# Block-causal attention with eight routed experts on one core: early row gathers in turns with weight pieces, and expert 3's rows gathered among the results

## The chip, the core and the metric

The kernel runs on one core of a Trainium2 chip: TensorE (matmul; in the profile PE, its weight loads PEld), VectorE (DVE), ScalarE (ACT), GpSimd (POOL) and SyncE (SP), and 16 DMA engines that all queues share. The metric is the time of one execution on the device in microseconds; smaller is better. The kernel before took 266.24 us, the median of three runs (264.31 to 266.30).

## The reference

Two stages. First, causal attention by blocks of 64: 8 batches, 8 heads, 576 positions, head size 64. Its result is laid out as 4608 token rows of 512 values. Second, each token row goes through the expert that `domain_id` names, one of 8:

```python
scores = np.where(block_i >= block_j, scale * q @ k.T, -1e9)   # blocks of 64 positions
x = softmax(scores) @ v        # -> rows (4608, 512)
...
for e in range(E):
    mask = domain_id == e
    h = np.maximum(x[mask] @ w1[e], 0.0)      # (512, 1024)
    out[mask] = h @ w2[e]                     # (1024, 512)
```

## The kernel before

**Attention** runs in 32 steps, one for a pair of heads that share a batch (`for p in range(npair + 1)`, L580). In a step TensorE makes scores, ScalarE exponentials (L398), TensorE the product with v (L435, L446), VectorE the normalisation into the tile `x` (L459). When four steps (a batch) are done, its rows are stored to a buffer in device memory, `x_rows` (`store_x`, L465), by SyncE's queue and partly ScalarE's.

**Routing** is worked out beside attention: a table `tok0` holds for each expert 5 blocks of 128 token numbers. It is built so that blocks 0 to 2 of an expert hold only tokens of the first five batches ("early" blocks), and blocks 3 and 4 the rest.

**Gathers.** Rows go from `x_rows` into an expert's tile `xg` (four buffers) by an indirect DMA of 128 rows that GpSimd issues. `early_gather` (L528) reads an early block with row numbers that `early_row` (L524) has copied; it waits only for the first five batches. `gather` (L489) waits for all stores. GpSimd also issues every load of weights (each expert has w1 and w2, each in two halves of 128 x 2 x 1024 or the like, converted from four bytes to two on the way, list `todo`) and every result, an indirect DMA that scatters 128 rows to the output (L735). So GpSimd's instruction list is one queue for rows, weights and results; what stands behind a waiting instruction waits too. Each of its DMAs also waits for the one eight places earlier.

**What sets the order around the change.** All is written out by hand. The dict `issue` (L574) tells what GpSimd issues at the end of attention step p: a pair (e, w) is the early gather of block w of expert e, any integer is the next piece of weights from `todo`. After step 31 the calls from L780 on follow: further early gathers, then late blocks of experts 0 to 2 in turns with weights (`run(...)`, L786), then the two matmul stages of experts 0 and 1. These two are cut in an early part (blocks 0 to 2, `mm1_part` and `mm2` with `range(NE)`) and a late part (blocks 3 and 4). `mm1_part` (L704) is rows times w1 with ReLU on ScalarE into `hT`; `mm2` (L717) is `hT` times w2, one block of 128 tokens at a time, copied to `osb` (ten buffers) and scattered. The dict that `mm2` gets lists what GpSimd issues behind each block's result.

**Turning rows.** Matmuls need the rows turned (`xT`, three buffers). For expert 0's early blocks TensorE does it in the last two attention steps (`early_blocks`, L510), for the others of experts 0 and 1 TensorE does it too (`transpose_block`, L670, `turn_late`, L767), and from expert 2 on VectorE, 16 transposes of 32 x 32 blocks for an expert (`turn`, L674). Experts 2 to 7 are a loop (L810): turn the next expert, then mm1 and mm2 of this one; results of expert e go in turns with rows and weights of later experts (`beside_results`, L756). The last loop (L821), for experts with more than 640 tokens, runs no round here.

Of the kernel before, what the change touches and what calls it, by code (L numbers as in the profile page):

```python
# [17 lines left out]
def kernel(  # L18
# [16 lines left out]
    NB = 5  # L35
# [5 lines left out]
    NE = 3  # L41
# [437 lines left out]
    def weights(e):  # L479
        where = (msb, 1) if e % (NW + 1) == NW else (wsb, NW)  # L480
        w1s[e], w2s[e], todo = load_weights(moe_w1[e], moe_w2[e], *where)
        return todo
# [6 lines left out]
    def gather(g, tok, blks):  # L489
        for blk in blks:  # L490
            nc.gpsimd.indirect_dma_start(  # L491
                out=g[:, blk, :], out_offset=None, in_=xd,
                in_offset=bass.IndirectOffsetOnAxis(
                    ap=tok[:, 1, blk : blk + 1], axis=0),
                bounds_check=N - 1, oob_is_err=False)

    def new_xg():
        return gsb.tile([128, NB, DM], F16, name="xg", tag="xg", bufs=4)
# [25 lines left out]
    def early_row(e, w):  # L524
        rows[e, w] = const.tile([128, 1], I32, name=f"row{e}{w}")
        nc.vector.tensor_copy(out=rows[e, w][:], in_=tok_of(e)[:, 1, w : w + 1])  # L526

    def early_gather(e, w):  # L528
        row = rows[e, w]
        nc.gpsimd.indirect_dma_start(  # L530
            out=xgs[e][:, w, :], out_offset=None, in_=xd[0 : N - LB * S],
            in_offset=bass.IndirectOffsetOnAxis(ap=row[:, 0:1], axis=0),
            bounds_check=N - LB * S - 1, oob_is_err=False)
# [32 lines left out]
    def turn_qk(*at):  # L566
        if at in Ts:
            G, s = Ts[at]
            if s == 0 and G > 1:
# [1 line left out]
            emit_T(G, s, beside.get(at[0]) if at[1] else None)  # L571

    prev, full, halves = None, [], []
    issue = {22: (0, 0), 24: ((0, 0), (0, 1)), 25: ((0, 2), 0), 26: ((1, 0), 0),  # L574
             27: ((1, 1), 0), 28: ((1, 2), 0), 30: ((2, 0),), 31: ((2, 1),)}

    def tok_of(e):
        return tok0[:, :, NB * e : NB * e + NB]

    for p in range(npair + 1):  # L580
# [63 lines left out]
            xgs = [new_xg() for _ in range(4)]  # L644
            xT = new_xT()
        if p == npair - 1:
            early_row(2, 2)
            for w in range(NE):
                early_row(3, w)
        for g in issue.get(p, ()):  # L650
            if isinstance(g, int):
                todo.pop(0)()
# [17 lines left out]
    def transpose_block(g, xT, blk):  # L670
        pt = new_po()[:, 0:256].bitcast(F16).rearrange("p (c n) -> p c n", c=4)
        transpose_to(pt, g, xT, blk)
# [91 lines left out]
    def dst_of(e):  # L764
        return outs[NB * e : NB * e + NB]

    def turn_late(g, xT):  # L767
        for blk in range(NE, NB):
            transpose_block(g, xT, blk)

    def rows_of(e, *blks):
        if len(xgs) <= e:
            xgs.append(new_xg())
        return [lambda blk=blk: gather(xgs[e], tok_of(e), (blk,)) for blk in blks]

    def run(*fs):
        for f in fs:
            f()

    early_gather(2, 2)  # L780
    W1, W2 = todo, weights(2)
    g0, g1, g2, g3 = (rows_of(e, *range(NE, NB)) for e in range(4))
    early_gather(3, 0)
    early_gather(3, 1)
    early_gather(3, 2)
    run(g0[0], W1[0], g0[1], W1[1], g1[0], W2[0], g1[1], g2[0], W2[1], g2[1])  # L786
    hT0, hT1, xT0, xT1, xT2 = new_hT(), new_hT(), xT, new_xT(), new_xT()
    mm1_part(xT0, hT0, w1s[0], 0, CE)
    mm2(hT0, w2s[0], tok_of(0), dst_of(0), range(NE),
        {0: [W2[2]], 1: [g3[0], W2[3]], 2: [g3[1]]},  # L790
        more={n: [lambda n=n: transpose_block(xgs[1], xT1, n)
                  for n in ((0,), (1, 2))[n]] for n in range(2)})
    mm1_part(xT1, hT1, w1s[1], 0, CE, lambda: turn_late(xgs[0], xT0))
# [1 line left out]
    W, g4 = weights(3), rows_of(4, *range(NB))  # L795
    mm1_part(xT0, hT0, w1s[0], CE, CAP - CE)
    mm2(hT0, w2s[0], tok_of(0), dst_of(0), range(NE, NB),
        {0: [g4[0], W[0]], 1: [g4[1], W[1]]})
    mm2(hT1, w2s[1], tok_of(1), dst_of(1), range(NE),
        {0: [g4[2], W[2]], 1: [g4[3], W[3]], 2: [g4[4]]},  # L800
        more={0: [lambda: turn_late(xgs[1], xT1)]})
    turn(xgs[2], xT2, NE, NB)
    mm1_part(xT1, hT1, w1s[1], CE, CAP - CE)
    W, g5 = weights(4), rows_of(5, 0, 1, 2)
# [71 lines left out]
```

## Time and profile before

| | |
|---|---|
| median of three runs (range) | 266.24 us (264.31 to 266.30) |
| the profiled execution | 264.74 us, span 263.0 us, granted TensorE clock 0.991 |
| TensorE busy | 246.5 us (94%) |
| VectorE, ScalarE, GpSimd busy | 179.4, 161.7, 170.0 us |
| GpSimd's DMA queue | 60192 packets, 45.63 MB |
| DMA rate, mean over the span | 193 GB/s |
| attention until about | 111.8 us |

The span is the time from the first to the last instruction; the run's own time is 1.7 us longer. Share of busy time is an average: attention and experts are two stages with different limits, so the views below are read by stretch of time. GpSimd's busy time in the profile is the time in which it writes a DMA's list, not the time of the transfer.

### The profile page before, as it was taken

To read this page: it belongs to the slowest core of one execution; us is meant where nothing else is said; L and a number is where in the kernel's file an instruction comes from. 1 tells how busy PE (TensorE), PEld (TensorE's weight loads), DVE (VectorE), ACT (ScalarE), POOL (GpSimd) and SP (SyncE) were. 2 spreads that over 40 slices of the span, in tenths; PEclk is the share of its full clock that TensorE was granted. 3 is DMA by queue.
4 is the path that set the end of the run, shared out by engine and by line. 5 is a ranking of instruction groups with operands and counts; after the bars stand their busy time and mean duration, and the time that the engine had idled before them with its cause. 6 is when DMAs were issued, how large, how long until landed. Compare 5 with 4: busy or idle time off the path is not lost. (4 is left out here: it accounts for less than half of the span.)

```text
span 263.0 us, 7025 instructions
## 1 busy us (share of the span) xinstructions
PE 246.5 (94%) x2918; PEld 156.6 (60%) x2918; DVE 179.4 (68%) x306; ACT 161.7 (62%) x201; POOL 170.0 (65%) x200
## 2 busy tenths in 40 slices
PE   7799999999999999898999999999999999999970
PEld 5466666666667666654565675564654745646540
DVE  4779998999977866511597899996959949600010
ACT  1669998999999889724443464463553644635420
POOL 8698965747485557365888888678888864042150
PEclk9999999999999999999999999999999999999996
DMA  5999999999999999994999999999999999022030
GB/s 79 156 171 183 208 176 228 188 214 197 204 214 198 209 204 260 251 268 73 218 241 275 211 262 259 228 258 238 264 207 258 224 230 289 27 100 80 2 149 34
DMA packets 65889, 50.85 MB, mean 193 GB/s; under 512 B 41277, under 2 KB 54077, under 8 KB 65856
## 3 DMA queue, kind: packets, MB, share of 16 engines
q0 software_dynamic: 60192, 45.63, 101.1%
q1 hardware_dynamic: 5120, 4.33, 6.1%
q8 instruction: 24, 0.39, 0.6%
q10 hardware_dynamic: 544, 0.43, 0.5%
q14 instruction: 9, 0.07, 0.1%
HBM read 67.15 MB, written 15.20 MB: 313 GB/s over the span
## 5 line engine op out<-in xcount | busy, mean ns | idle before, releaser
L398 ACT ACTIVATE A<-ps 128x1024 f16<-128x1024 f32 x96 | 92.2, 1023 | 11.2 <-PE ps L393 4.3
L679 DVE STREAM_TRANSPOSE xT<-xg 32x640 f16<-32x640 f16 (+2 forms) x112 | 82.9, 741 | 11.3 <-DMA xg<-x_rows,tok 7.4
L725 PE MATMUL po<-w2h,hT 128*128 128x512 f16 (+1 forms) x328 | 71.4, 374 | 0.7 <-DMA xg<-x_rows,row 0.6
L735 POOL DMA_INDIRECT out_dram<-osb,tok x40 | 40.5, 1013 | 36.4 <-ACT osb L732 22.1
L725 PEld LDWEIGHTS <-hT 128*128 128x128 f16 x328 | 31.8, 98 | 36.3 <-ACT hT L714 1.7
L696 PE MATMUL ph<-xT,w1h 128*128 128x320 f16 x384 | 53.1, 299 | 0.1
L732 ACT COPY osb<-po 128x512 f32<-128x512 f32 (+1 forms) x39 | 22.6, 581 | 45.6 <-PE po L725 37.5
L696 PEld LDWEIGHTS <-w1h 128*128 128x128 f16 x384 | 37.6, 98 | 15.8 <-issue 0.4
L700 ACT ACTIVATE hT<-ph 128x640 f16<-128x640 f32 x48 | 33.8, 704 | 19.1 <-PE ph L696 15.0
L383 DVE COPY QK<-PT 128x1152 f16<-128x1152 f16 x30 | 40.5, 1351 | 4.5 <-PE ps L393 1.5
L393 PE MATMUL ps<-QK 64*128 64x64 f16 (+3 forms) x320 | 39.0, 295 | 1.8 <-ACT A L398 1.1
L95 POOL DMA_DIRECT2D vS<-in_v_dram x44 | 35.7, 831 | 3.1 <-DMA kh<-in_k_dram 1.6
L491 POOL DMA_INDIRECT xg<-x_rows,tok x28 | 29.1, 1039 | 12.0 <-issue 6.4
L435 PE MATMUL po<-vS,A 128*128 128x65 f16 x640 | 28.9, 195 | 1.3 <-DVE x L459 1.0
L435 PEld LDWEIGHTS <-A 128*128 128x128 f16 x640 | 23.1, 98 | 10.6 <-issue 7.9
L459 DVE TENSOR_TENSOR x<-po,rc 128x640 f16<-128x640 f32 x32 | 26.4, 824 | 1.1
L446 PE MATMUL po<-vS,A 64*64 64x65 f16 (+1 forms) x320 | 21.0, 194 | 0.4 <-DMA vS<-in_v_dram 0.3
L730 DVE COPY osb<-po 128x512 f32<-128x512 f32 (+1 forms) x2 | 1.1, 558 | 26.5 <-issue 25.5
L530 POOL DMA_INDIRECT xg<-x_rows,row x12 | 12.3, 1028 | 9.6 <-DVE row L526 5.2
L711 PE MATMUL ph<-xT,w1h 128*128 128x384 f16 (+1 forms) x128 | 18.4, 299 | 0.1
L76 POOL DMA_DIRECT2D qh<-in_q_dram x15 | 11.0, 731 | 11.2 <-DMA kh<-in_k_dram 9.5
L714 ACT ACTIVATE hT<-ph 128x768 f16<-128x768 f32 (+1 forms) x16 | 11.1, 704 | 11.1 <-PE ph L711 8.7
(109 smaller groups left out, 192.2 us busy)
## 6 DMA issues: line engine op xcount, KB each, us to landing
w1h<-in_moe_w_dram POOLq DMA_DIRECT2D x16, 512.0 KB
w2h<-in_moe_w_dram POOLq DMA_DIRECT2D x16, 512.0 KB
qh<-in_q_dram POOLq DMA_DIRECT2D x15, 288.0 KB
kh<-in_k_dram POOLq DMA_DIRECT2D x15, 288.0 KB
x_rows<-x SPq DMA_DIRECT2D x6, 512.0 KB
vS<-in_v_dram POOLq DMA_DIRECT2D x24, 128.0 KB
vS<-in_v_dram POOLq DMA_DIRECT2D x24, 64.0 KB
out_dram<-osb,tok POOLq DMA_INDIRECT x40
```

What stands on the lines that cost most here:

```text
L95: nc.gpsimd.dma_start(out=vS[b % RV][r0:128, c, h0:h1, 16:80], in_=v[b, h0:h1, 128 * c : 128 * c + n, :].rearrange("h p d -> p h d"))
L383: nc.vector.tensor_copy(out=QKs[G][:, s].rearrange("p i (n j) -> p i n j", j=R), in_=P16.rearrange("p (j i n) -> p i n j", j=R, i=2))
L393: nc.tensor.matmul(out=o[:, t], lhsT=QK[h, 1, i, 128 * c : 128 * c + 128], rhs=QK[h, 0, i, q0:q1], start=True, stop=True)
L398: nc.scalar.activation(out=o, in_=i, func=AF.Exp, scale=0.125)
L435: nc.tensor.matmul(out=po[:, t, 65 * w : 65 * w + 65], lhsT=st["A"][:, t, n0 : n0 + 128], rhs=vS[b % RV][:, c, head(st, t), 15:80], start= ...
L459: nc.vector.tensor_tensor(out=st["x"][:, :, c0 : c0 + 256].rearrange("p w (t i z) -> p i t w z", t=2, i=2)[:, st["i"]], in0=po[:, :, 0:325 ...
L491: nc.gpsimd.indirect_dma_start(out=g[:, blk, :], out_offset=None, in_=xd, in_offset=bass.IndirectOffsetOnAxis(ap=tok[:, 1, blk : blk + 1], ...
L679: nc.vector.transpose(out=dst[32 * j : 32 * j + 32, i, b0:b1], in_=src[32 * i : 32 * i + 32, j, b0:b1])
L696: nc.tensor.matmul(out=ph[:, i, 0:w], lhsT=w1_cols(w1h, dc, fc), rhs=xT[:, dc, w * i : w * i + w], start=(dc == 0), stop=(dc == 3))
L700: nc.scalar.activation(out=hT[:, fc, :].rearrange("p (i n) -> p i n", i=2), in_=ph[:, :, 0:w], func=AF.Relu)
L725: nc.tensor.matmul(out=po[:, 0:w], lhsT=hT[:, fc, 128 * blk : 128 * blk + 128], rhs=w2h[:, fc, w * i : w * i + w], start=(fc == 0), stop=( ...
L735: nc.gpsimd.indirect_dma_start(out=dst[blk], out_offset=bass.IndirectOffsetOnAxis(ap=tok[:, 0, blk : blk + 1], axis=0), in_=osb[:], in_off ...
```

## The change

It changes three things, and no arithmetic.

1. `issue`: in steps 24 to 28 one early gather and one piece of weights stand in each step. The first half of expert 0's w1 stays in step 22, the second goes from there behind the first early gather; expert 0's third block and all of experts 1 and 2 follow one step or place later than before.
2. Expert 3 loses its three early gathers after step 31 (and the copies of their row numbers); expert 2's second block joins the third there.
3. Expert 3 gets all five blocks by ordinary gathers behind the results of experts 0 and 1 (`g3` has five entries), and expert 4's five blocks follow behind them.

```diff
--- before.py
+++ after.py
@@ -571,8 +571,8 @@
             emit_T(G, s, beside.get(at[0]) if at[1] else None)
 
     prev, full, halves = None, [], []
-    issue = {22: (0, 0), 24: ((0, 0), (0, 1)), 25: ((0, 2), 0), 26: ((1, 0), 0),
-             27: ((1, 1), 0), 28: ((1, 2), 0), 30: ((2, 0),), 31: ((2, 1),)}
+    issue = {22: (0,), 24: ((0, 0), 0), 25: ((0, 1), 0), 26: ((0, 2), 0),
+             27: ((1, 0), 0), 28: ((1, 1), 0), 30: ((1, 2),), 31: ((2, 0),)}
 
     def tok_of(e):
         return tok0[:, :, NB * e : NB * e + NB]
@@ -644,9 +644,8 @@
             xgs = [new_xg() for _ in range(4)]
             xT = new_xT()
         if p == npair - 1:
-            early_row(2, 2)
-            for w in range(NE):
-                early_row(3, w)
+            for w in (1, 2):
+                early_row(2, w)
         for g in issue.get(p, ()):
             if isinstance(g, int):
                 todo.pop(0)()
@@ -777,17 +776,16 @@
         for f in fs:
             f()
 
+    early_gather(2, 1)
     early_gather(2, 2)
     W1, W2 = todo, weights(2)
-    g0, g1, g2, g3 = (rows_of(e, *range(NE, NB)) for e in range(4))
-    early_gather(3, 0)
-    early_gather(3, 1)
-    early_gather(3, 2)
+    g0, g1, g2, g3 = (
+        rows_of(e, *range(NE if e < 3 else 0, NB)) for e in range(4))
     run(g0[0], W1[0], g0[1], W1[1], g1[0], W2[0], g1[1], g2[0], W2[1], g2[1])
     hT0, hT1, xT0, xT1, xT2 = new_hT(), new_hT(), xT, new_xT(), new_xT()
     mm1_part(xT0, hT0, w1s[0], 0, CE)
     mm2(hT0, w2s[0], tok_of(0), dst_of(0), range(NE),
-        {0: [W2[2]], 1: [g3[0], W2[3]], 2: [g3[1]]},
+        {0: [g3[0], W2[2]], 1: [g3[1], W2[3]], 2: [g3[2]]},
         more={n: [lambda n=n: transpose_block(xgs[1], xT1, n)
                   for n in ((0,), (1, 2))[n]] for n in range(2)})
     mm1_part(xT1, hT1, w1s[1], 0, CE, lambda: turn_late(xgs[0], xT0))
@@ -795,9 +793,9 @@
     W, g4 = weights(3), rows_of(4, *range(NB))
     mm1_part(xT0, hT0, w1s[0], CE, CAP - CE)
     mm2(hT0, w2s[0], tok_of(0), dst_of(0), range(NE, NB),
-        {0: [g4[0], W[0]], 1: [g4[1], W[1]]})
+        {0: [g3[3], W[0]], 1: [g3[4], W[1], g4[0]]})
     mm2(hT1, w2s[1], tok_of(1), dst_of(1), range(NE),
-        {0: [g4[2], W[2]], 1: [g4[3], W[3]], 2: [g4[4]]},
+        {0: [g4[1], W[2], g4[2]], 1: [g4[3], W[3]], 2: [g4[4]]},
         more={0: [lambda: turn_late(xgs[1], xT1)]})
     turn(xgs[2], xT2, NE, NB)
     mm1_part(xT1, hT1, w1s[1], CE, CAP - CE)
```

On GpSimd, at attention steps 22 to 30 (L530 is an early gather, L127 and L132 are halves of w1 and w2, expert 0's, then expert 1's w1). Before:

```order
L127 DMA w1h_2051<-in_moe_w1_dram 128x2x1024 x2
L530 DMA xg_2229<-x_rows,row00_2234 128x512
L530 DMA xg_2229<-x_rows,row01_2239 128x512
L530 DMA xg_2229<-x_rows,row02_2316 128x512
L132 DMA w2h_2052<-in_moe_w2_dram 128x2x1024
L530 DMA xg_2230<-x_rows,row10_2393 128x512
L132 DMA w2h_2052<-in_moe_w2_dram 128x2x1024
L530 DMA xg_2230<-x_rows,row11_2471 128x512
L127 DMA w1h_2227<-in_moe_w1_dram 128x2x1024
L530 DMA xg_2230<-x_rows,row12_2552 128x512
L127 DMA w1h_2227<-in_moe_w1_dram 128x2x1024
```

And now:

```order
L127 DMA w1h_2051<-in_moe_w1_dram 128x2x1024
L530 DMA xg_2228<-x_rows,row00_2233 128x512
L127 DMA w1h_2051<-in_moe_w1_dram 128x2x1024
L530 DMA xg_2228<-x_rows,row01_2311 128x512
L132 DMA w2h_2052<-in_moe_w2_dram 128x2x1024
L530 DMA xg_2228<-x_rows,row02_2388 128x512
L132 DMA w2h_2052<-in_moe_w2_dram 128x2x1024
L530 DMA xg_2229<-x_rows,row10_2466 128x512
L127 DMA w1h_2226<-in_moe_w1_dram 128x2x1024
L530 DMA xg_2229<-x_rows,row11_2547 128x512
L127 DMA w1h_2226<-in_moe_w1_dram 128x2x1024
L530 DMA xg_2229<-x_rows,row12_2670 128x512
```

The second half of w1 stands behind the first early gather, and each gather of experts 0 and 1 behind a piece of weights.

On GpSimd, from step 31 to the first late blocks (L491 is a gather that waits for all stores of attention rows; `xg_2231` before and `xg_2230` now are expert 2's rows, `xg_2229` now expert 1's). Before, six early gathers stand here from step 30 on, the last three for expert 3 (`xg_2232`):

```order
L530 DMA xg_2231<-x_rows,row20_2675 128x512
L530 DMA xg_2231<-x_rows,row21_2751 128x512
L530 DMA xg_2231<-x_rows,row22_2743 128x512
L530 DMA xg_2232<-x_rows,row30_2745 128x512
L530 DMA xg_2232<-x_rows,row31_2747 128x512
L530 DMA xg_2232<-x_rows,row32_2749 128x512
L491 DMA xg_2229<-x_rows,tok0_149 128x512
L132 DMA w2h_2228<-in_moe_w2_dram 128x2x1024
```

And now:

```order
L530 DMA xg_2229<-x_rows,row12_2670 128x512
L530 DMA xg_2230<-x_rows,row20_2742 128x512
L530 DMA xg_2230<-x_rows,row21_2738 128x512
L530 DMA xg_2230<-x_rows,row22_2740 128x512
L491 DMA xg_2228<-x_rows,tok0_149 128x512
L132 DMA w2h_2227<-in_moe_w2_dram 128x2x1024
```

Those of expert 3 are gone, expert 1's last early block has come in with step 30, and the first L491 stands two places nearer.

On GpSimd, from the first result of expert 0 on (L735, and L734 in the changed kernel, is a result; `xg_2232` before and `xg_2231` now are expert 3's rows, `xg_3019` and `xg_3007` expert 4's; `w1h_3017` and `w1h_3005` are expert 3's w1). Before:

```order
L735 DMA out_0_dram<-osb_2881,tok0_149 4608x512
L132 DMA w2h_2805<-in_moe_w2_dram 128x2x1024
L735 DMA out_0_dram<-osb_2902,tok0_149 4608x512
L491 DMA xg_2232<-x_rows,tok0_149 128x512
L132 DMA w2h_2805<-in_moe_w2_dram 128x2x1024
L735 DMA out_0_dram<-osb_2932,tok0_149 4608x512
L491 DMA xg_2232<-x_rows,tok0_149 128x512
L735 DMA out_0_dram<-osb_3060,tok0_149 4608x512
L491 DMA xg_3019<-x_rows,tok0_149 128x512
L127 DMA w1h_3017<-in_moe_w1_dram 128x2x1024
L735 DMA out_0_dram<-osb_3078,tok0_149 4608x512
L491 DMA xg_3019<-x_rows,tok0_149 128x512
```

And now, behind the first result:

```order
L491 DMA xg_2231<-x_rows,tok0_149 128x512
L132 DMA w2h_2799<-in_moe_w2_dram 128x2x1024
L734 DMA out_0_dram<-osb_2890,tok0_149 4608x512
L491 DMA xg_2231<-x_rows,tok0_149 128x512
L132 DMA w2h_2799<-in_moe_w2_dram 128x2x1024
L734 DMA out_0_dram<-osb_2920,tok0_149 4608x512
L491 DMA xg_2231<-x_rows,tok0_149 128x512
L734 DMA out_0_dram<-osb_3048,tok0_149 4608x512
L491 DMA xg_2231<-x_rows,tok0_149 128x512
L127 DMA w1h_3005<-in_moe_w1_dram 128x2x1024
L734 DMA out_0_dram<-osb_3066,tok0_149 4608x512
L491 DMA xg_2231<-x_rows,tok0_149 128x512
```

Expert 3's rows are five in place of two, its last stands where expert 4's second stood with one row more ahead of it, and expert 4's are behind.

## Rows read from the trace of the kernel before

**Rows 1.** TensorE's waits, 100 to 175 us: us in total, times, longest

```profile
PE po L725 <- DMA xg<-x_rows,row: 0.6, 1, 0.6
PE po L505 <- DMA xg<-x_rows,tok: 0.6, 1, 0.6
...
PE po L725 <- ACT hT L714: 0.2, 1, 0.2
```

**Rows 2.** TensorE in time: start us, us, what, [idle before, releaser]

```profile
109.43 0.61 PE L515 MATMUL PT<-identh,xg 128*128 128x128 f16 x8
...
118.86 0.61 PE L725 MATMUL po<-w2h,hT 128*128 128x512 f16 x2 [0.57 <-DMA xg<-x_rows,row]
119.64 0.60 PE L725 MATMUL po<-w2h,hT 128*128 128x512 f16 x2 [0.18 <-ACT hT L714]
...
127.74 0.40 PE L505 MATMUL po<-identh,xg 128*128 128x128 f16 x4 [0.55 <-DMA xg<-x_rows,tok]
...
167.90 8.86 PE L696 MATMUL ph<-xT,w1h 128*128 128x320 f16 x64
...
185.23 8.86 PE L696 MATMUL ph<-xT,w1h 128*128 128x320 f16 x64
```

**Rows 3.** ScalarE in order of time, end of attention

```profile
117.99 1.59 ACT L714 ACTIVATE hT<-ph 128x768 f16<-128x768 f32 x2 [2.08 <-issue]
```

**Rows 4.** GpSimd in order of time, from the last early rows on

```profile
111.34 1.01 POOL L530 DMA_INDIRECT xg<-x_rows,row  x1 [2.82 <-DVE row L526]
...
116.57 1.00 POOL L530 DMA_INDIRECT xg<-x_rows,row  x1 [0.31 <-issue]
120.86 1.00 POOL L491 DMA_INDIRECT xg<-x_rows,tok  x1 [3.29 <-DMA x_rows<-x]
...
122.94 1.04 POOL L491 DMA_INDIRECT xg<-x_rows,tok  x1 [0.30 <-issue]
```

**Rows 5.** SyncE's queue in order of time, its last store

```profile
114.10 0.59 SPq L469 DMA_DIRECT2D x_rows<-x  x1
```

**Rows 6.** four stretches: busy time by engine, granted clock, DMA share, GB/s

```profile
115.00:116.00 1.00, 0.88 (x7) 0.43 (x5) 0.00 (x0) 0.81 (x1) 0.74 (x1) 1.00 1.10 326
116.00:117.00 1.00, 1.00 (x7) 0.61 (x7) 0.00 (x0) 0.00 (x0) 0.69 (x2) 1.00 0.95 291
117.00:118.00 1.00, 1.00 (x7) 0.42 (x5) 0.00 (x0) 0.01 (x1) 0.57 (x1) 1.00 0.75 238
119.00:120.00 1.00, 0.82 (x4) 0.21 (x3) 0.00 (x0) 0.58 (x1) 0.00 (x0) 1.00 0.15 55
```

**Rows 7.** GpSimd in order of time, first weights and early rows

```profile
90.91 0.72 POOL L127 DMA_DIRECT2D w1h<-in_moe_w_dram  x1 [0.72 <-DMA qh<-in_q_dram]
93.60 1.10 POOL L530 DMA_INDIRECT xg<-x_rows,row  x1 [1.97 <-DMA x_rows<-x]
...
97.08 1.00 POOL L530 DMA_INDIRECT xg<-x_rows,row  x1 [0.30 <-issue]
...
103.23 0.76 POOL L127 DMA_DIRECT2D w1h<-in_moe_w_dram  x1 [0.89 <-DMA w1h<-in_moe_w_dram]
```

**Rows 8.** GpSimd in order of time, rows among the results

```profile
145.08 1.04 POOL L491 DMA_INDIRECT xg<-x_rows,tok  x1 [0.30 <-issue]
...
155.49 1.04 POOL L491 DMA_INDIRECT xg<-x_rows,tok  x1 [0.30 <-issue]
...
189.70 1.04 POOL L491 DMA_INDIRECT xg<-x_rows,tok  x1 [0.30 <-issue]
...
206.24 1.05 POOL L491 DMA_INDIRECT xg<-x_rows,tok  x1 [0.30 <-issue]
```

**Rows 9.** VectorE in order of time, transposes of experts 3 to 7

```profile
150.74 27.19 DVE L679 STREAM_TRANSPOSE xT<-xg 32x640 f16<-32x640 f16 x32 [0.91 <-DMA xg<-x_rows,tok]
...
196.90 13.58 DVE L679 STREAM_TRANSPOSE xT<-xg 32x640 f16<-32x640 f16 x16 [2.97 <-DMA xg<-x_rows,tok]
214.02 2.53 DVE L679 STREAM_TRANSPOSE xT<-xg 32x640 f16<-32x640 f16 x3 [3.54 <-DMA xg<-x_rows,tok]
```

## The prediction

> **What bounds the kernel now.** I read the profile from the engine that is busiest down to the queue that feeds it. First TensorE's waits from 100 to 175 us, the stretch in which the change acts: three lines, 0.6, 0.6 and 0.2 us [rows 1]. From there on the engine hardly stops, so nothing that is freed elsewhere is worth more than these lines. Then the order of time for TensorE [rows 2]: it stood 0.57 us before 118.86 and 0.18 us a little later (within expert 0's first results), and 0.55 us before 127.74 (turning the last block of expert 0's rows). The first has two names in the profile: the table of waits names a row DMA, but the matmul there reads only expert 0's hidden values and w2, and ScalarE wrote the third piece of those values at 117.99 after standing 2.08 us with no releaser shown [rows 3]. So I put 0.57 + 0.18 = 0.75 us down to ScalarE. The second is a real DMA wait: the last late block of expert 0, issued by GpSimd at 122.94 [rows 4], was usable at 127.74, 4.8 us later.
>
> Why was it issued so late? GpSimd stood 3.29 us until 120.86 for the last stores of attention rows [rows 4], which SyncE had issued by 114.10 + 0.59 = 114.69 [rows 5]. Until past 116 us the DMA engines were full (share 1.10 at 115 to 116, 326 GB/s), the share was 0.75 at 117 to 118 and 0.15 at 119 to 120 [rows 6]. The stores ended with the drained queue, and among what was drained were the early rows issued from 111.34 to 116.57 [rows 4], three of which are expert 3's and needed only after 150 us.
>
> **The change part by part.** *Three early rows of expert 3 go from the end of attention.* Each is 128 rows of 512 two-byte values, 131 KB, together 0.39 MB; at 326 GB/s (115 to 116 us [rows 6]) that is 1.2 us, at 291 (116 to 117) 1.35. I take 1.3 us as the time by which the stores land earlier. The bounds are 0 (the stores end by their own pace) and 5.5 us (GpSimd, now through with its early rows at 111.34 + 3 x 1.31 = 115.3, finds them landed); the row nearest is the queue's own rate, since transfer and stores lie together in it. Everything on GpSimd behind the wait moves up by 1.3. The block of 122.94 then lands at 126.4, TensorE asks for it at 127.74 - 0.55 = 127.19: the stall of 0.55 goes, with 0.75 us to spare. ScalarE's 0.75 us I leave: no instruction of ScalarE moves, and 2.08 us without a releaser may come again. Bounds for it: 0 and -0.75.
>
> The Trainium skill's page DMA: Bandwidth & Descriptors, section Queues, rings and completion order, speaks against the 1.3: each DMA engine takes its queue rows in turn, packet by packet, so a store on SyncE's row gets its share however many rows GpSimd has queued. By that rule alone the saving is nearer to 0 than to 1.3; that the stores were among the last to end [rows 4, 6] neither proves nor refutes it, since half of a busy engine is still slower than all of it.
>
> *Three copies of row numbers on VectorE go*: they stood in its pause before the first results. Nothing.
>
> *Early rows in turns with weights.* The second half of expert 0's w1 moves from 90.91 behind the first early row, which waited until 93.60 for stored rows [rows 7]: it is issued near 94.7. A half of w1 took at the longest 12.3 us: the one issued at 90.91 released GpSimd at 103.23 [rows 7] (eight DMAs later). It lands by 107.0; mm1 of expert 0 begins after 109.43 [rows 2]. Nothing. Expert 0's third row moves from 97.08 behind the first half of w2, one piece (0.76 + 0.30 [rows 7]) later: 98.1. TensorE turns it at 109.43, 11.3 us after. Rows took 4.8 to 7.8 us where a wait shows it (below). Nothing, but it becomes a rival if it takes the 12.3 us of a weight piece. Experts 1 and 2 have more slack: their rows are turned after 118.86 [rows 2].
>
> *Expert 3's five rows among the results.* GpSimd's queue grows by three rows of 1.04 + 0.30 = 1.34 us, 4.0 us in all, in a stretch in which it stands only 0.30 us between instructions [rows 8]: no pause takes them up. Expert 3's last row now stands one row behind the place where expert 4's second stood (145.08 [rows 8]): 146.4, less 1.3, 145.1. Latency there: VectorE waited until 196.90 for a row issued at 189.70 (7.2 us) and until 214.02 for one of 206.24 (7.8 us) [rows 8, 9]. So it lands at 152.3 to 152.9. VectorE began expert 3's transposes at 150.74 (behind its read of the round count, not the rows), 32 in 27.19 us, 13.6 for an expert [rows 9]; TensorE starts expert 3 at 167.90 [rows 2]. Latest start 154.3, or 153.75 with TensorE 0.55 earlier: 0.85 to 1.45 us to spare. So the transposes start 1.6 to 2.2 us later and nobody waits; that is the thinnest cover here. Expert 4: its last row moves from 155.49 [rows 8] to 155.49 + 4.0 - 1.3 = 158.2, lands by 166.0, is turned behind expert 3 by 180.1; TensorE wants it at 185.23 - 0.55 [rows 2]. From expert 5 on the rows come at most 2.7 us later, where 196.90 + 13.58 = 210.5 [rows 9] stands before a start at 219.9 (185.23 and two more experts of 185.23 - 167.90 = 17.33 us each). GpSimd's results come 2.7 us later too, but nothing waits: ten buffers take them.
>
> Sum against the profiled execution: 264.74 - 0.55 = **264.19 us** (span 263.0 to 262.45). That execution lies 1.5 us under the median of 266.24 and 0.6 under the middle (265.3) of the runs shown, so I name 264.8 for a measured time.
>
> **Rivals.** *Same as before.* The stores land when they did, by their own queue's pace; the stall at 127.74 stays. For it: the stores were issued as late as 114.69, behind nothing but their own data. Against it: full engines until 117. 264.74, or 265.3 in the middle of the runs. The page's rule on turns between queue rows would give this.
>
> *Expert 3 starves: slower.* Its last row decides at a latency of 153.75 - 145.1 = 8.65 us. Above it VectorE starts late and TensorE stands before expert 3 by the same amount. For it: GpSimd and the DMA share (about 1.1) are both full there, and 12.3 us was seen [rows 7]; that end costs 3.65 us. Against: 7.2 and 7.8 in the later stretch. Half way, 10.5 us, costs 1.85: 264.74 - 0.55 + 1.85 = 266.0. The same page, section Anatomy of one DMA, fits 2.0 us plus bytes over 436 GB/s, an estimate of 2.3 us for such a row, which would close this rival; the rows measure 4.8 to 7.8, so I keep it.
>
> *Expert 0's third row is late*: at 12.3 us it lands at 110.4 for 109.43, 1.0 us, so 264.74 - 0.55 + 1.0 = 265.2.
>
> *Both stalls go*: 264.74 - 1.30 = 263.44, if ScalarE's pause depends on the full DMA engines; this is the lower end of my forecast.
>
> **How the numbers follow.** Forecast 0.58 (a fourth of it both stalls), same as before 0.22, expert 3 starves 0.13, third row late 0.07. The runs of the kernel before lie 0.43 under to 1.56 over the profiled execution; the forecast's own range is 264.74 - 1.30 - 0.43 = 263.0 to 264.19 + 1.56 = 265.8. "Same" reaches 266.3 and the starving rival starts near 266, so the range for 8 in 10 is 263.0 to 266.5. One per cent, about what this measurement can tell from no change, is 2.7 us. Faster by more needs both stalls gone and a low run, or a stall that is larger in other executions than in this one: 0.13. Slower by more needs the starving rival in its upper half: 0.05. Within 1%: 0.82.
>
> **What would show it.** GpSimd's wait for the stores ends near 119.6; no wait of TensorE for late rows of expert 0; ScalarE's pause at 116 to 118 either there or not; VectorE starts expert 3 near 152.6 and waits for rows; TensorE starts expert 3 0.5 us earlier, counted from the end of attention, with no wait. I am wrong if the stores still land near 120.9, or if TensorE shows a wait before expert 3 or before 109.43.

## The result and the profile after

The changed kernel took 268.05 us (median of 13 runs, 265.44 to 269.16), the kernel before, beside it, 265.46 us (13 runs, 263.31 to 269.60). The ratio is 1.0096, 95% interval 1.0069 to 1.0123: 1% slower, where 264.8 us and a small gain were forecast; the time lies outside the range. A ratio here compares only each kernel's fast runs, those within 1.5% of its own fastest, so that a kernel with a wide spread loses more of them (3 of the 13 of before, none of after) and the ratio can lie some tenths of a per cent from that of the medians, which is given below where the two part most. The profiled execution of after took 268.37 us (span 266.6, mean granted clock 0.978), that of before 264.74 (263.0, 0.991).

First TensorE's waits from 100 to 240 us (us in total, times, longest):

```profile
PE po L505 <- DMA xg<-x_rows,tok: 2.4, 1, 2.4
PE ph L695 <- ACT hT L699: 1.0, 1, 1.0
```

The late row of expert 0 that had cost 0.55 us [rows 1, 2] costs 2.4, the two waits at 118 to 120 us that the prediction put down to ScalarE are gone, and a new one by ScalarE stands in the loop over the experts. GpSimd in order of time, from its last early row to expert 0's last late block, and SyncE's last store:

```profile
114.31 1.00 POOL L530 DMA_INDIRECT xg<-x_rows,row  x1 [0.31 <-issue]
120.69 1.00 POOL L491 DMA_INDIRECT xg<-x_rows,tok  x1 [5.38 <-DMA x_rows<-x]
...
122.77 1.04 POOL L491 DMA_INDIRECT xg<-x_rows,tok  x1 [0.30 <-issue]
```

```profile
114.47 0.59 SPq L469 DMA_DIRECT2D x_rows<-x  x1
```

Its early rows end 2.26 us earlier (116.57 before, 114.31 now), as the edit says, but the wait for the stores ends at 120.69 in place of 120.86 [rows 4]: the wait got longer, 5.38 us for 3.29. Times from the start of the span mislead a little here, since this execution also issued its last store later, at 114.47 for 114.10 [rows 5]: from that issue to GpSimd's release it took 6.22 us, for 6.76, which is 0.54 us less where 1.3 were forecast. TensorE in order of time, first before, then now:

```profile
111.77 5.65 PE L711 MATMUL ph<-xT,w1h 128*128 128x384 f16 x32
...
126.80 0.39 PE L505 MATMUL po<-identh,xg 128*128 128x128 f16 x4
...
127.97 6.44 PE L711 MATMUL ph<-xT,w1h 128*128 128x384 f16 x48
...
150.58 8.85 PE L696 MATMUL ph<-xT,w1h 128*128 128x320 f16 x64
...
228.58 8.80 PE L725 MATMUL po<-w2h,hT 128*128 128x512 f16 x40
```

```profile
112.33 5.49 PE L710 MATMUL ph<-xT,w1h 128*128 128x384 f16 x32
...
126.11 0.39 PE L505 MATMUL po<-identh,xg 128*128 128x128 f16 x4
128.86 0.61 PE L505 MATMUL po<-identh,xg 128*128 128x128 f16 x4 [2.37 <-DMA xg<-x_rows,tok]
129.26 7.75 PE L710 MATMUL ph<-xT,w1h 128*128 128x384 f16 x48
...
152.87 8.86 PE L695 MATMUL ph<-xT,w1h 128*128 128x320 f16 x64
...
170.20 8.86 PE L695 MATMUL ph<-xT,w1h 128*128 128x320 f16 x64
...
226.80 5.59 PE L695 MATMUL ph<-xT,w1h 128*128 128x320 f16 x40 [0.96 <-ACT hT L699]
232.23 8.80 PE L724 MATMUL po<-w2h,hT 128*128 128x512 f16 x40
```

The block issued at 122.77 is turned at 128.86, 6.1 us later (before: 4.8). The 48 matmuls behind it take 7.75 us; before they took 6.44. The stretches say why (columns as in [rows 6]; the last three numbers are granted clock, DMA share, GB/s):

```profile
117.00:118.00 1.00, 1.00 (x8) 0.59 (x6) 0.00 (x0) 0.39 (x2) 0.00 (x0) 1.00 0.68 230
119.00:120.00 1.00, 1.00 (x9) 0.57 (x8) 0.19 (x1) 0.42 (x1) 0.00 (x0) 1.00 0.03 9
128.00:129.00 1.00, 0.14 (x2) 0.14 (x3) 0.00 (x0) 0.00 (x0) 0.69 (x2) 0.75 1.08 197
129.00:130.00 1.00, 1.00 (x7) 0.65 (x6) 0.50 (x2) 0.00 (x0) 1.00 (x2) 0.50 1.08 229
131.00:132.00 1.00, 1.00 (x5) 0.44 (x4) 0.99 (x2) 0.00 (x0) 0.69 (x2) 0.55 1.15 207
132.00:133.00 1.00, 1.00 (x8) 0.59 (x6) 0.97 (x3) 0.81 (x1) 0.83 (x1) 1.00 1.16 270
```

At 117 to 118 the DMA share is a little lower than before (0.68 for 0.75), at 119 to 120 nearly nothing moves (9 GB/s for 55); yet the stores' completion reached GpSimd only 0.17 us sooner. And after TensorE's pause the clock stands at its lower level, 1.2 GHz, until about 132 us: the 48 matmuls lose 1.3 us. VectorE's start of expert 3, and ScalarE at expert 6, in order of time:

```profile
154.85 27.19 DVE L678 STREAM_TRANSPOSE xT<-xg 32x640 f16<-32x640 f16 x32 [2.58 <-DMA out_dram<-osb,tok]
```

```profile
223.75 0.70 ACT L699 ACTIVATE hT<-ph 128x640 f16<-128x640 f32 x1 [0.52 <-ACT osb L731]
226.04 1.30 ACT L699 ACTIVATE hT<-ph 128x640 f16<-128x640 f32 x2 [1.58 <-PE ph L695]
```

Expert 3's transposes begin 4.1 us later than before (150.74 [rows 9]); 13.6 us for expert 3 end at 168.45, TensorE starts it at 170.20, so nobody waits. TensorE itself came to expert 2 2.29 us later, so what it kept in hand before expert 3 shrank by only 1.8. At expert 6 ScalarE leaves the second ReLU until 226.04, though TensorE had run ahead; TensorE then waits 0.96 us.

The two executions differ by 3.63 us, and from these starts it adds up. TensorE begins expert 0's first matmuls 0.56 us later (112.33 for 111.77; attention's, ahead of all that the change touches: between 12 and 16 us the granted clock was 0.50 to 0.72 here and 1.00 before). From there to the turning of the late block it gains 1.25: ScalarE's 0.75 is gone, and some smaller gaps. That brings it to the late block sooner, and counted from those first matmuls the block was issued 0.73 sooner but took 1.29 us longer to be usable: 1.25 - 0.73 + 1.29 = 1.81. So it loses 1.81 more for the late block, 1.47 to the clock with the start of the matmuls behind it, and a gap of 0.30 before expert 2 is gone: +2.29 at expert 2 (152.87 for 150.58). Expert 3 starts at +2.30 and expert 4 at +2.29. ScalarE's late starts at experts 4 and 6 add the rest, +3.65 at expert 6's second stage (232.23 for 228.58), and it stays so to the end.

### The profile page after: what moved, and what is told of

It reads as the page before. It is cut to its first block, busy times and chain, and to the rows that moved or that the text cites. A ratio compares the mean times of both kernels' runs of the same rounds, so it can differ in the third digit from the quotient of the medians.

```text
span 266.6 us, 7022 instructions
## 1 busy us (share of the span) xinstructions
PE 249.0 (93%) x2918; PEld 157.9 (59%) x2918; DVE 178.8 (67%) x303; ACT 161.7 (61%) x201; POOL 170.0 (64%) x200
## 5 line engine op out<-in xcount | busy, mean ns | idle before, releaser
L734 POOL DMA_INDIRECT out_dram<-osb,tok x40 | 40.5, 1012 | 36.5 <-ACT osb L731 23.0
L491 POOL DMA_INDIRECT xg<-x_rows,tok x31 | 32.2, 1038 | 15.0 <-issue 7.3
L710 PE MATMUL ph<-xT,w1h 128*128 128x384 f16 (+1 forms) x128 | 19.6, 312 | 0.0
L76 POOL DMA_DIRECT2D kh<-in_k_dram x15 | 10.9, 725 | 10.7 <-DMA qh<-in_q_dram 5.1
```

Source lines behind the costliest of these rows:

```text
L491: nc.gpsimd.indirect_dma_start(out=g[:, blk, :], out_offset=None, in_=xd, in_offset=bass.IndirectOffsetOnAxis(ap=tok[:, 1, blk : blk + 1], ...
L734: nc.gpsimd.indirect_dma_start(out=dst[blk], out_offset=bass.IndirectOffsetOnAxis(ap=tok[:, 0, blk : blk + 1], axis=0), in_=osb[:], in_off ...
```

## The experiments

Each call ran on one chip of its own, with the kernel before beside it; chips differ in level and in habits, so only ratios within a call are compared. I call the chips A to D; on which one the result was measured is not on record. On A and B no profile of the unchanged kernel was taken; where their profiles are set against before, it is the one of the result.

### Which part carries the loss: chip A (before 266.11 us)

**Only the new order of early rows and weights**: the dict `issue` of after, while expert 3 keeps its three early rows.

```diff
-    issue = {22: (0, 0), 24: ((0, 0), (0, 1)), 25: ((0, 2), 0), 26: ((1, 0), 0),
-             27: ((1, 1), 0), 28: ((1, 2), 0), 30: ((2, 0),), 31: ((2, 1),)}
+    issue = {22: (0,), 24: ((0, 0), 0), 25: ((0, 1), 0), 26: ((0, 2), 0),
+             27: ((1, 0), 0), 28: ((1, 1), 0), 30: ((1, 2),), 31: ((2, 0),)}
```

> The order of attention steps 22 to 31 alone (weights and early gathers in turns); expert 3 keeps its three early gathers. Theory 1 (the loss comes from expert 3's rows among the results: they land about 34 us after the store wait ends, and 13.6 us of transposes stand between them and TensorE): as before, ratio 0.997 to 1.003; VectorE starts expert 3 behind its read of the round count. Theory 2 (the loss comes from the late block of expert 0 meeting TensorE earlier, one long pause and a fall of the granted clock): the same pause can come here, ratio 1.004 to 1.010, with no wait of VectorE for expert 3. Theory 3 (the new order itself delays the stores or the weights): ratio about 1.010.

Measured: 265.36 us, 0.9987 (0.9947 to 1.0027): nothing. TensorE in time has ScalarE's pauses, as before has them, and no wait for expert 0's late block:

```profile
115.49 1.46 PE L712 MATMUL ph<-xT,w1h 128*128 128x384 f16 x8 [0.80 <-issue]
118.35 0.60 PE L726 MATMUL po<-w2h,hT 128*128 128x512 f16 x2 [0.54 <-issue]
119.84 0.60 PE L726 MATMUL po<-w2h,hT 128*128 128x512 f16 x2 [0.89 <-ACT hT L715]
```

**Only expert 3's rows among the results**: the second and third part of the change, with the old `issue`.

```diff
-    g0, g1, g2, g3 = (rows_of(e, *range(NE, NB)) for e in range(4))
-    early_gather(3, 0)
...
+    g0, g1, g2, g3 = (
+        rows_of(e, *range(NE if e < 3 else 0, NB)) for e in range(4))
...
+        {0: [g3[0], W2[2]], 1: [g3[1], W2[3]], 2: [g3[2]]},
```

> Expert 3's five rows among the results alone; the order of steps 22 to 31 stays as before. Theory 1: carries the whole loss, ratio 1.006 to 1.012, VectorE starts expert 3 three to four us later than before and waits for rows; TensorE stands before expert 3 in executions without a pause for expert 0's late block. Theory 2: ratio 1.000 to 1.005. Theory 3: ratio 0.997 to 1.003.

Measured: 267.26 us, 1.0076 (1.0041 to 1.0112); by the medians 1.0043. On this chip there is a loss with this part alone. VectorE began expert 3 at 152.67, 1.9 us later than before and not the three to four expected, and TensorE did not wait for it. TensorE in time:

```profile
128.05 0.40 PE L505 MATMUL po<-identh,xg 128*128 128x128 f16 x4 [1.61 <-DMA xg<-x_rows,tok]
...
224.95 1.25 PE L694 MATMUL ph<-xT,w1h 128*128 128x320 f16 x8 [1.15 <-issue]
226.45 4.51 PE L694 MATMUL ph<-xT,w1h 128*128 128x320 f16 x32 [0.26 <-ACT hT L698]
```

The pauses at 115 to 120 us are gone, the late block costs more, so it starts expert 2 level with before (150.59 for 150.58); 2.2 us are lost from expert 4 to expert 6, all while ScalarE starts late.

**One line: both late blocks of expert 0 ahead of the half of w2**, in after and in before.

```diff
-    run(g0[0], W1[0], g0[1], W1[1], g1[0], W2[0], g1[1], g2[0], W2[1], g2[1])
+    run(g0[0], g0[1], W1[0], W1[1], g1[0], W2[0], g1[1], g2[0], W2[1], g2[1])
```

> The changed kernel with expert 0's second late block issued ahead of the half of w2 that stood before it. No pause of TensorE in turning expert 0's late blocks under every theory (the block then lands near 125). Theory 1: the time won there is given back before expert 3, TensorE stands 2 to 3 us there, ratio to before 1.005 to 1.012, no faster than the changed kernel by more than 1 us. Theory 2: all comes back, ratio 0.990 to 0.998. Theory 3: ratio 1.000 to 1.008.

> The kernel before with the same swap, expert 0's second late block ahead of the half of w2. Theory 1 and 2: the pause of 0.55 us goes, and with it the longer ones and the falls of the clock in other executions: ratio 0.990 to 0.998, since expert 3's rows have about 5 us to spare. Theory 3: ratio 0.997 to 1.000.

Measured: after with it 265.79 us, 1.0024 (0.9982 to 1.0067); before with it 264.53 us, 0.9982 (0.9947 to 1.0017), by the medians 0.9988 and 0.9941. The ratio of after with the swap lies between the bands of theories 1 and 2. In both the wait for the late block is gone. In after, TensorE comes to expert 3 at 165.8, and there the cover that the prediction called thinnest is used up; first TensorE, then VectorE in time:

```profile
165.81 8.85 PE L695 MATMUL ph<-xT,w1h 128*128 128x320 f16 x64 [1.19 <-DVE xT L678]
...
223.06 1.25 PE L695 MATMUL ph<-xT,w1h 128*128 128x320 f16 x8 [0.95 <-issue]
```

```profile
152.08 22.93 DVE L678 STREAM_TRANSPOSE xT<-xg 32x640 f16<-32x640 f16 x27 [5.49 <-DMA xg<-x_rows,tok]
```

So in the result the pause for the late block hid that expert 3's rows come late. ScalarE's pause at expert 6 is there again: after, the rows alone and after with the swap show 0.95 to 1.15 us of it, while before and the new order alone show none and before with the swap 0.40. The pauses at 115 to 120 us divide the six kernels the other way.

### Do three rows less free the stores: chip B (before 268.93 us)

**Before without expert 3's three early rows** (zeros stand in their place, so part of expert 3 isn't computed).

```diff
-    early_gather(3, 0)
-    early_gather(3, 1)
-    early_gather(3, 2)
+    nc.vector.memset(xgs[3][:, 0:NE, :], 0.0)
```

> The kernel before with expert 3's three early gathers left out and nothing in their place: zeros stand in those three blocks, so this part of expert 3 is not computed. GpSimd's later queue is as in the kernel before. It gives the pure gain of taking the rows away from the end of attention. My sum of the prediction: GpSimd's wait for the stores ends 1.3 us earlier. Theory A (the stores end by their own pace, and ScalarE's pause at 116 to 119 hangs on what GpSimd and the DMA engines do there): the wait ends at most 0.6 us earlier, ScalarE's pause is under 0.5 us in place of 2, ratio 0.990 to 0.997, no pause of ScalarE at expert 6. Theory B (ScalarE's pauses are chance): pause as in the kernel before, ratio 0.997 to 1.002.

Measured: 269.44 us, 1.0015 (0.9965 to 1.0065). SyncE's last store and GpSimd, then TensorE, in time:

```profile
114.85 0.59 SPq L469 DMA_DIRECT2D x_rows<-x  x1
```

```profile
121.09 1.00 POOL L491 DMA_INDIRECT xg<-x_rows,tok  x1 [6.41 <-DMA x_rows<-x]
```

```profile
129.33 0.40 PE L505 MATMUL po<-identh,xg 128*128 128x128 f16 x4 [2.58 <-DMA xg<-x_rows,tok]
129.57 6.44 PE L709 MATMUL ph<-xT,w1h 128*128 128x384 f16 x48
```

The rows are gone altogether and GpSimd is still released at 121.1, for 120.86 in the result's profile of before. But this execution issued its last store at 114.85, 0.75 us later than that one, and it ran on another chip. Counted from the last store's issue to GpSimd's release the rows do cost something. One number for each profile, but for the run below that issues weights into the wait (us):

| chip | expert 3's early rows there | not there |
|---|---|---|
| A, and the result | 6.76, 7.51, 6.47 | 6.22, 6.29, 6.83 |
| B | 8.32, 8.62, 8.42 | 6.24, 7.12, 6.49, 8.08 |
| C | 8.45, 7.27 | 6.98, 7.06 |
| D | 9.15 | 7.75 |

The means are 7.9 and 6.9. Part of the scatter is the time of issue: the later the last store is issued, the shorter the time. A straight-line fit that allows for that and for the chip leaves 0.75 us to the rows, with a standard error of 0.2. So the stores don't end wholly by their own pace. The forecast's first term had the right sign and was too large: 1.3 for 0.54 in the result's own pair. The saving brought nothing here, for TensorE waited 2.58 us for the late block, 6.2 us after its issue. The ratio lies in theory B's band, but none of this call's profiles shows ScalarE's pause, so it can't judge between the theories.

**GpSimd 4 us late**: before, with 13 short instructions behind the third row gather among expert 3's results, which is one of expert 7's (the lines that hand the longer list on are left out).

```diff
+            g[2:3] = g[2:3] + [lambda: nc.gpsimd.iota(
+                out=pace[:], pattern=[[1, 128]], base=0, channel_multiplier=0)] * 13
```

> The kernel before with 13 small index instructions (about 0.3 us each, no DMA) put into GpSimd's queue behind the third row gather among expert 3's results: its last results and expert 7's weights come about 4 us later, as in the changed kernel, and nothing else moves. Theory A (a late GpSimd queue costs time at expert 6, where its run of results and the last weights then lie beside expert 6's ReLU work and ScalarE starts late): ScalarE pauses 1 to 2 us at expert 6, ratio 1.004 to 1.009. Theory B (the pauses at expert 6 are chance or come from expert 3's rows): no pause there, ratio 0.998 to 1.002.

Measured: 268.63 us, 0.9936 (0.9882 to 0.9990). By the medians the ratio is 0.9989. No loss from a late GpSimd, but neither this nor any other profile of this chip shows ScalarE's pauses, so it can't tell whether those hang on GpSimd. Nor was GpSimd as late as meant: the 13 instructions take 3.88 us, but TensorE was late itself. GpSimd issued the last half of expert 7's w2 7.4 us ahead of TensorE's start of expert 6; it was 8.4 in before and 4.7 to 6.5 in the three kernels with the pause at expert 6. The two repeats below have 6.8 and 7.6.

**After with expert 7's w2 later**, both halves among expert 5's results:

```diff
+        if e + 4 == E:
+            late[:], w = w[2:], w[:2]
```

> The changed kernel with both halves of expert 7's w2 issued among expert 5's results in place of expert 4's: GpSimd catches up with its results about 2 us earlier, before expert 6's ReLU work. Theory A: ScalarE's pause of 1.3 us at expert 6 goes or shrinks below 0.5 us, 1 to 1.5 us faster than the changed kernel, ratio to before 1.003 to 1.006. Theory B: as the changed kernel, ratio about 1.010.

**The same, with the first half of expert 1's w2 ahead of the wait and both late blocks directly behind it**:

```diff
-    run(g0[0], W1[0], g0[1], W1[1], g1[0], W2[0], g1[1], g2[0], W2[1], g2[1])
+    run(W1[0], g0[0], g0[1], W1[1], g1[0], W2[0], g1[1], g2[0], W2[1], g2[1])
```

> The changed kernel with three edits: the first half of expert 1's w2 is issued while GpSimd waits for the stores, both late blocks of expert 0 directly behind the wait, and expert 7's w2 among expert 5's results. GpSimd's queue behind the wait is 0.8 to 1.1 us shorter than in the changed kernel. If the stores do not land later: no pause for expert 0, wait before expert 3 of 0 to 1 us, pause at expert 6 under 0.5 us, ratio 0.988 to 0.998. If the half of w2 takes DMA time from the stores: the wait ends 1 to 2 us later and all that is behind it too, expert 3's wait stays, ratio 0.998 to 1.005.

Measured: 266.51 us, 0.9916 (0.9879 to 0.9954), and 266.48, 0.9895 (0.9813 to 0.9976). The first came out faster than either theory said. In the second GpSimd waits for the stores until 124.94, 10.02 us after the last was issued, the longest of all profiles: here weights put into the idle queue delayed what the wait is for. Its ratio is nevertheless that of the branch without delay. Its second late block, directly behind the first, is turned 2.99 us after its issue. After itself wasn't in this call, so the later w2's own part isn't separated.

### Is the loss there on other chips: chips C (before 267.54 us) and D (268.24 us)

**Before and after once more**, unchanged, on C:

> The kernel before once more, for a profile on the chip of the three runs beside it. Every theory: ratio 1.000 within 0.003. It shows which pauses this chip has: of TensorE before expert 0's late block, of ScalarE at 116 to 119 and at expert 6.

> The changed kernel once more on the same chip. Theory A (expert 3's rows land later: VectorE starts expert 3 two to four us later, a floor under TensorE's start of expert 3; and the late GpSimd queue meets expert 6's ReLU work): slower by 0.5 to 1 per cent on a chip where ScalarE pauses, within 0.5 per cent on a chip without such pauses and with a long pause before expert 0's late block. Theory C (the chip decides only the level, the change costs the same everywhere): ratio 1.007 to 1.012 on any chip.

Measured: before against itself 1.0113 (1.0022 to 1.0205, four runs), by the medians 1.0075; after 1.0006 (0.9964 to 1.0048). On D, with more rounds:

> The changed kernel once more. Theory (the change itself is worth about nothing; the 1% of the result came from TensorE's pause for expert 0's late block, whose length differs between executions of either kernel, and from ScalarE's late starts, which only some chips show): 0.994 to 1.006 on a chip without ScalarE's pauses, 1.004 to 1.010 on one with them. Rival (the loss belongs to the change on every chip): 1.007 or more, whatever ScalarE shows.

> The kernel before against itself, to see how far two copies of one program lie apart: 0.996 to 1.004 if the interval tells all of the scatter, up to 1% from 1 if it does not, as in the first such run (1.0113 from four runs).

Measured: after 267.47 us, 1.0003 (0.9958 to 1.0049); before against itself 0.9995 (0.9942 to 1.0049). On two further chips the change shows no cost, with intervals that reach about 0.5% either way (by the medians 0.9971 on both). TensorE in the repeat of before on C, and in that of after on D:

```profile
130.06 0.61 PE L505 MATMUL po<-identh,xg 128*128 128x128 f16 x4 [6.21 <-DMA xg<-x_rows,tok]
130.46 8.92 PE L711 MATMUL ph<-xT,w1h 128*128 128x384 f16 x48
```

```profile
129.39 0.40 PE L505 MATMUL po<-identh,xg 128*128 128x128 f16 x4 [4.28 <-DMA xg<-x_rows,tok]
129.62 8.12 PE L710 MATMUL ph<-xT,w1h 128*128 128x384 f16 x48
```

The kernel before can lose 6.2 us at the place where I read 0.55, and 2.5 more to the clock. No profile of C or D has a pause by ScalarE.

**GpSimd 4 us late once more**, on C:

> The kernel before with GpSimd's queue 4 us later from expert 3's results on, again, beside a profile of the kernel before on this chip. Theory A: ScalarE pauses 1 to 2 us at expert 6 where this chip shows ScalarE pauses elsewhere, ratio 1.004 to 1.009; without such pauses on this chip 0.998 to 1.002. Theory B (pauses at expert 6 do not hang on GpSimd's lateness): no pause at expert 6, ratio 0.998 to 1.002.

Measured: 268.10 us, 1.0039 (1.0001 to 1.0078), a little above the band for a chip without pauses, and again without ScalarE's pause. After itself has none in this call either, though it issued expert 7's last half of w2 only 4.8 us ahead of expert 6: a late GpSimd alone does not bring the pause on this chip.

**After with the swap of the late block and the later w2 of expert 7**, on C:

> The changed kernel with expert 0's second late block ahead of the half of w2, and expert 7's w2 among expert 5's results. No pause for expert 0; a wait of 1 to 2 us before expert 3 stays; the pause at expert 6 goes under theory A. Ratio to before 0.988 to 0.998, about the kernel before with the first of the two edits alone; under theory B 0.998 to 1.003.

Measured: 262.95 us (four runs), 0.9892 (0.9792 to 0.9993), by the medians 0.9828, against 1.0006 for after in the same call.

### What is left of the change without the late block's wait: chip B again (before 268.06 us)

The rows alone and the late GpSimd, the same files as above (the 13 instructions again stand among expert 3's results, not behind expert 3's own rows):

> Expert 3's five rows among the results, alone, a second time on whatever chip comes. Theory 1 (the loss of this part is paid through ScalarE's late starts at experts 4 to 6, which only some chips show): with such pauses in its profile 1.006 to 1.011 again, without them 0.998 to 1.003. Rival (the loss is paid in TensorE's pause for expert 0's late block): 1.004 or more also where ScalarE shows no pause, and a pause for that block that is longer than 2 us.

> Before, with 13 short instructions more on GpSimd (about 4 us) behind expert 3's first gather among the results; expert 3's early rows stay. Theory 1a (ScalarE's pause at expert 6 comes with a GpSimd queue that runs late): on a chip whose rows3_only_2 has the pause, this kernel has it too, 0.5 to 1.5 us, ratio 1.002 to 1.006. Rival 1b (the pause comes from somewhere else, the rows themselves): no pause here, ratio 0.998 to 1.002, while rows3_only_2 has it.

Measured: 267.05 us, 0.9927 (0.9887 to 0.9967), for the rows alone, which lost 0.76% on chip A, below both theories' bands; 0.9935 (0.9885 to 0.9985) for the late GpSimd. Neither has a pause by ScalarE, so this pair decides nothing on what brings it. A pure delay reads 0.65% under before, twice on this chip, and that is not in the medians (268.73 for 268.06 us here, 268.63 for 268.93 the first time); the rows alone read 0.9962 by the medians. So differences of that size are not to be read from one ratio here.

**Before and after, both with the swap and the later w2**:

> Before, with expert 0's second late block issued ahead of the half of w2, and both halves of expert 7's w2 among expert 5's results. Theory 2 (the pause for the late block is the loss that can be taken out, and the change's moves bring nothing): 0.988 to 0.996, at or under swap_late_2. Rival (the change's moves are worth something once the late block no longer waits): 0.5% or more above swap_late_2.

> The changed kernel with the same two edits, a second time. Theory 2: 0.988 to 0.997, TensorE without a pause for expert 0's late block and with 1.0 to 1.7 us before expert 3, where the rows among the results end last. Rival (its gain on the other chip was that chip's): 0.998 or more.

Measured: before so 263.62 us, 0.9835 (0.9792 to 0.9879); after so 263.96 us, 0.9847 (0.9803 to 0.9891). Both are some 1.6% faster than before; after was not in this call, elsewhere it came out between 1.0003 and 1.0096 of before. Between the two the intervals overlap: no gain of the change shows. How much of the 1.6% is the swap's and how much the later w2's is not separated: after with the later w2 alone read 0.9916 on this chip, before with the swap alone 0.9982 on A. Before with the two edits, GpSimd and TensorE in time:

```profile
121.29 0.99 POOL L491 DMA_INDIRECT xg<-x_rows,tok  x1 [4.65 <-DMA x_rows<-x]
122.59 1.00 POOL L491 DMA_INDIRECT xg<-x_rows,tok  x1 [0.31 <-issue]
```

```profile
125.62 0.40 PE L505 MATMUL po<-identh,xg 128*128 128x128 f16 x4 [0.98 <-DMA xg<-x_rows,tok]
125.86 6.44 PE L711 MATMUL ph<-xT,w1h 128*128 128x384 f16 x48
...
150.16 8.85 PE L696 MATMUL ph<-xT,w1h 128*128 128x320 f16 x64 [1.83 <-DMA xg<-x_rows,tok]
```

The stores still end at 121.3, but the second late block, directly behind the first, is turned 3.0 us after its issue, and the clock doesn't fall. The next wait is 1.83 us before expert 2, by its releaser for rows too. TensorE of after with the same edits:

```profile
124.29 0.40 PE L505 MATMUL po<-identh,xg 128*128 128x128 f16 x4 [0.56 <-DMA xg<-x_rows,tok]
...
148.77 8.85 PE L695 MATMUL ph<-xT,w1h 128*128 128x320 f16 x64 [1.78 <-DVE n_i L751]
...
168.06 8.85 PE L695 MATMUL ph<-xT,w1h 128*128 128x320 f16 x64 [1.80 <-DVE xT L678]
```

It has one wait more, the 1.80 us before expert 3, whose rows stand among the results.

## Why the prediction was wrong, point by point

- **"The block of 122.94 then lands at 126.4 ... the stall of 0.55 goes": the step that failed.** The block was usable at 128.86 and the stall grew to 2.37 us. I carried the 4.8 us from issue to use over from one execution as if it were fixed. It measured 6.1 in after, and 5.15 to 7.45 in the other profiles in which TensorE waited for a late block behind the 512 KB half of w2; directly behind the first block it measured 3.0. In the kernel before itself the wait runs from 0.55 to 6.2 us, from one execution to another. The clock's fall behind it (1.3 us here, up to 2.5) had no term at all, since the profile of before shows none at this place. My sum also kept TensorE's request at 127.19, though with ScalarE's pauses and some smaller gaps gone it comes 1.25 us sooner, counted from its first matmuls of expert 0. "Same" and the other rivals had no longer latency either; the one sentence on a stall that differs between executions counted it as a gain only. That 1.0096 still falls within the 1% to which I gave 0.82 is luck: no term of the sum points that way.
- **"Everything on GpSimd behind the wait moves up by 1.3": right sign, mis-sized.** It moved up by 0.17 us in the span, and by 0.54 counted from the last store's issue, which came 0.37 us later in that execution. Over nineteen profiles the rows are worth about 0.75. I took the early rows and the stores for one drained queue. The rule of the Trainium skill that spoke against it (page DMA: Bandwidth & Descriptors, section Queues, rings and completion order) has each engine take its queue rows in turn. The traces agree with that in part: the saving lies between 0 and the 1.3 of a queue that must drain first, 0.54 in the result's pair and 0.75 over all. Taking turns leaves a store its share of an engine and not the whole of it, so the rule does not by itself give the rival "same", as I let it. My sign of being wrong, stores that land near 120.9, came true at 120.69, but a time within the span could not tell a smaller saving from none.
- **ScalarE's 0.75 us, left as it was:** it went (the lower bound), but a pause of 0.96 us at expert 6 and a smaller delay at expert 4 came, 1.36 us in all, for which the sum had no term.
- **"GpSimd's results come 2.7 us later too, but nothing waits":** not refuted, not shown. On A the loss of 0.76% (0.43% by the medians) is with expert 3's rows and lies where ScalarE starts late; on B, C and D kernels with the rows so moved show no loss. What makes ScalarE start late, with no releaser in the trace, stays open; delaying GpSimd was only tried on chips that don't show it, and there by less against TensorE than meant.
- **"The transposes start 1.6 to 2.2 us later and nobody waits":** they started 4.1 us later, and nobody waited by luck, because the pause ahead made TensorE late too. With that pause shortened or taken out the rival "expert 3 starves" is real: 1.19, 1.45, 1.64 and 1.80 us in four profiles, of the 1.85 priced.
- **Early rows in turns with weights, nothing:** right, 0.9987 alone, and no wait for expert 0's third row.
- **The copies of row numbers, nothing:** no wait appeared, not tried alone.

How much of the 1.0096 is the change's is settled only so far: 1.0003 and 1.0006 on two other chips, 1.0076 (by the medians 1.0043) for its second and third part on A. The cause of the whole 1% stays open. In the two profiles of the result 3.28 us of loss are the late block and the clock behind it, which differ as much between executions of one kernel.

## What to carry to other kernels

A stall read from one execution is a sample: before pricing its removal, ask what sets its length, here the 512 KB transfer issued ahead of a 131 KB one that TensorE needs first, and change that order. To see what emptying a queue does for a wait, count from the issue of what is waited for, over several executions: by the span's clock the stores ended 0.17 us sooner, from their issue 0.54, and 0.75 over nineteen profiles. A cover of 1 us is not slack but the next bound, and becomes visible as soon as the stall ahead of it goes.

## What the runs showed of the hardware

- From the last store's issue to GpSimd's release it took 6.2 to 8.1 us without three 131 KB gathers on GpSimd's queue, 6.5 to 9.2 with them, and 10.0 in the one profile with a 512 KB load of weights issued into the wait.
- A gather of 128 rows was usable 3.0 us after its issue directly behind another one, and 4.8 to 7.45 us behind a 512 KB load of weights.
- The granted clock fell to 0.50 around TensorE's pause for the late block after 2.37 us in one profile and 3.33 to 6.21 in eight others, but not after 2.58 and 3.25 (48 matmuls in 6.44 us, against 7.75 to 8.92).
- Late starts of ScalarE that the trace doesn't explain, 0.2 to 1.2 us of TensorE each, stand in all six profiles of chip A and of the result, and in none of the 14 from the three other chips.
- The same program's median differed by call, 265.5 to 268.9 us for before (268.9 and 268.1 in two calls on one chip), and four runs against 19 of the same program read 1.0113, with an interval that leaves out 1.
